# Scores of the first two batches as one float32 product per head half-array, q and k transposed whole

## The chip, the core and the metric

One core of one Trainium2 chip runs the whole program. The metric is the time of one execution on the device in microseconds. The core has a matrix engine (TensorE, PE, with PEld for its weight loads), a vector engine (VectorE, DVE), an activation engine (ScalarE, ACT), a general engine (GpSimd, POOL) and a queue engine that here issues all DMAs (SyncE, SP). Each engine runs its own instructions in the order that the program gives them.

## What is computed

Attention with a top-32 mask, then two dense stages. q, k and v have shape (4, 8, 576, 64): batches, heads, rows, channels.

```
scores = 0.125 * q @ k.T                      # 576 x 576 per batch and head
kth    = the 32nd largest of each row
attn   = softmax over the scores >= kth
x      = attn @ v                             # heads side by side: (4, 576, 512)
# dense stage 1: mixes with the row before, relu(xk @ w_k)^2 @ w_v, times sigmoid(xr @ w_r)
# dense stage 2: gelu(x @ w_in), layer norm of one half, w_sg over the rows, @ w_out, + x
```

The change touches the first line alone, and how q and k get into the layout that it needs.

## The kernel before, in words

**Work and order.** A pair of heads of one batch is a "super" (16 pairs; in batch 0, `HALVED`, each pair is done in two supers of 256 and 320 query rows, so there are 20). A super is cut into slots of 128 query rows; the fifth slot of a pair holds the last 64 rows of both heads. There are 80 slots, 20 to a batch. For each slot the loop at L873 does this: some pieces of preparation for the next super, `emit_S` for the slot two ahead, `emit_topk` for this slot (a search on DVE: L275 and L276 fold a row of 576 into maxima and minima, then MAX8 at L284 and MATCH_REPLACE8 at L294 four rounds), and between its rounds the mask of the slot before (L311), its transposes (`emit_T`) and, at a unit's end, the product with v (`emit_unit`). Into this the dense work of the batch before is spread by a quota, and in slots 0 to 24 the conversion of the float64 weights into pairs of f32r (`conv`, L488 to L497, on ACT, POOL and DVE). A priority is given to each block with `at(...)`, and a list scheduler makes the order of every engine from these. What is left of the dense work of the last batch runs behind the last slot.

**S before.** `load_raw` (L135) brings q and k into `rawq` and `rawk`, in which the blocks 0 to 3 are head 0, 4 to 7 head 1, and 8 the last 64 rows of both. `prep_pieces` (L160) makes the operands: ACT copies to f32r (the high part, L100 and L174), POOL subtracts that from the source (the low part, L102 and L175), so that high and low part of 64 channels fill 128 columns; PE transposes each block (L200, L208, L213, L218), ACT copies the result out of PSUM (L202, L209, L215, L220). `emit_S` (L232) multiplies in two f32r passes over 128 rows (high with both, low with both):

```
for a in range(2):
    for hf in range(2):
        nc.tensor.matmul(ps[:, hf, :HALF], lhsT=su.qst[h, t.u.ch][:, a, ...], rhs=su.kst[h][...], start=(a == 0), stop=(a == 1))
nc.scalar.activation(t.S[:, h].rearrange("p (a n) -> p a n", a=2), ps[:, :, :HALF], AF.Copy)
```

So there are eight products of 288 columns and two copies to a slot, a head at a time, through one PSUM tile (`BUFS["S"] = 1`). The slot with the last rows takes ten products (L253) and one copy (L255). The columns of head 1 are turned by 64, with the remainder first, as the later steps expect.

`split` at L98 is the helper of all high and low parts, of weights (`w`), activations (`xm`, `ksq`, ...) and k (`splk`, `splr`); by its lines L100 and L102 alone they can't be told apart, by the tile names they can.

Of the kernel before, what the change touches and what calls it, by code (L numbers as in the profile page):

```python
# [9 lines left out]
F32 = mybir.dt.float32  # L10
# [3 lines left out]
AF = mybir.ActivationFunctionType  # L14
# [9 lines left out]
def computation(ctx, tc, dram, wscr, flag, fast, q, k, v, mu_k, mu_r, w_k, w_v, w_r, w_in, g_ln, w_sg, b_sg, w_out, out):  # L24
    nc = tc.nc
    B, H, S, D = q.shape
# [7 lines left out]
    HALF = S // 2  # L34

    const = ctx.enter_context(tc.tile_pool(name="const", bufs=1))
    sb = ctx.enter_context(tc.tile_pool(name="sb", bufs=1))
# [65 lines left out]


    HALVED = (0,)

    class Rec:
        pass
# [26 lines left out]
    def load_raw(su, names):  # L135

        b, p = su.b, su.p
        for nm in names:
            if len(nm) == 1:
                nms = [(nm, h, part) for h in range(2) for part in range(2)]  # L140
            else:
                nms = [nm]
            for nm, h, part in nms:
                src = {"q": q, "k": k, "v": v}[nm]
                if nm not in su.raw:
                    su.raw[nm] = sb.tile([128, 9, D], F32, tag="raw" + nm, name="raw" + nm,
                                         bufs=2 if nm == "v" else 1)
                t = su.raw[nm]
                hd = src[b, 2 * p + h]
                if part:  # L150
                    if nm != "q" or 1 in su.chs:
                        nc.sync.dma_start(t[64 * h:64 * h + 64, 8, :], hd[512:])
                elif nm == "q":
                    for c in su.chs:
                        nc.sync.dma_start(t[:, 4 * h + 2 * c:4 * h + 2 * c + 2, :],
                                          hd[256 * c:256 * c + 256].rearrange("(p r) d -> p r d", r=2))
                else:
                    nc.sync.dma_start(t[:, 4 * h:4 * h + 4, :], hd[:512].rearrange("(p r) d -> p r d", r=4))

    def prep_pieces(su):  # L160

        su.kst, su.qst = {}, {}
        pieces = []
        has1 = 1 in su.chs
# [64 lines left out]
    def emit_S(t):  # L232
        su = t.su
        t.S = sb.tile([128, t.hs, S], F32, tag="S2", name="S2", bufs=3)
        for h in range(t.hs):
            ps = bank("S", (128, 2, 512))
            if t.j < 4:
# [596 lines left out]
    for i, t in enumerate(slots):  # L834
        if t.last and t.su.p == NP - 1:
# [3 lines left out]
            elif t.u.ch == 1:  # L839
# [2 lines left out]

    start = at(-100000)
    start.__enter__()
    load_raw(supers[0], [("k", 0, 0), ("q", 0, 0), ("k", 0, 1), ("k", 1, 1), ("k", 1, 0), ("q", 1, 0), ("q", 0, 1),
                         ("q", 1, 1)])
    for pc in prep_pieces(supers[0]):
        pc()
    for key in list(convq)[:4]:
# [138 lines left out]
```

## Time and profile before

| | us |
|---|---|
| median of 3 runs | 1001.49 (997.75 to 1002.79) |
| the profiled execution | 997.91 |
| its span, first to last instruction | 995.8 |
| DVE busy | 841.0 |
| PE busy | 878.1 |
| POOL busy | 528.7 |

The busy times are sums over the span. A slot's search is a run of DVE instructions; the order of the other engines is built around it. PE's busy time is that of pipelined products whose ends are modelled, so that a stretch in which PE is always busy still need not be one at PE's peak; idle time of PE is real. Durations of one form of instruction differ between stretches, which the tables by form show.

### The profile page before, as it was taken

How to read it: one execution, taken by the hardware profiler on the slowest of the kernel's cores; microseconds unless marked ns; L12 is line 12 of the kernel's file. 1: busy time of each engine (PE TensorE's matmuls, PEld its weight loads, DVE VectorE, ACT ScalarE, POOL GpSimd, SP SyncE). 2: the span in 40 equal slices, each digit the busy share in tenths (PEclk: the TensorE clock that was granted, in tenths of full speed). 3: DMA queues.
4: the chain of work that ended last, by engine and by line, in shares of the span. 5: the costliest groups of instructions: out<-in, count | busy, mean ns of one | idle time of the engine just before them, and what ended most of it. 6: DMA issues, size and time to landing. Idle time of an engine off the chain costs nothing.

```text
span 995.8 us, 18647 instructions
## 1 busy us (share of the span) xinstructions
PE 878.1 (88%) x6078; PEld 759.7 (76%) x6078; DVE 841.0 (84%) x2337; ACT 697.6 (70%) x1559; POOL 528.7 (53%) x630
## 2 busy tenths in 40 slices
PE   3465768889888989798999999989999998999997
PEld 2344547777778888577888979868999886899895
DVE  6899999998999999999999999999999973712142
ACT  6778878888886796677687679666876585554340
POOL 7788788675975168559343216598331125210051
PEclk9986779999999999988999999999999999999999
DMA  7953486888467645512333343354333436664432
GB/s 214 371 187 136 156 252 224 282 279 304 167 209 252 219 120 188 171 33 69 109 100 110 110 143 94 99 192 151 109 118 109 128 124 223 218 248 148 122 126 68
DMA packets 105067, 166.34 MB, mean 167 GB/s; under 512 B 19328, under 2 KB 74368, under 8 KB 104960
## 3 DMA queue, kind: packets, MB, share of 16 engines
q1 hardware_dynamic: 104960, 165.05, 50.8%
q8 instruction: 50, 0.82, 0.3%
q14 instruction: 57, 0.47, 0.1%
HBM read 134.27 MB, written 30.21 MB: 165 GB/s over the span
## 4 chain that ended last, share of the span: by engine, by line
PE 45%; DVE 28%; ACT 10%; DMA 8%; POOL 4%; issue 3%; SPq 2%; POOLq 0%; DVEq 0%; ACTq 0%
PE d L569 9%; DVE M L284 8%; PE d L634 6%; DVE E L311 6%; DVE T L294 6%; PE d L679 5%; PE S L240 3%; PE d L760 3%; DVE T L275 3%; PE d L788 3%; PE tp L569 3%; DVE T L276 2%; PE tp L326 2%; PE tp L355 2%; ACT E L306 2%
## 5 line engine op out<-in xcount | busy, mean ns | idle before, releaser
L284 DVE MAX8 M<-T 128x8 f32<-128x208 f32 (+3 forms) x576 | 261.2, 485 | 1.0
L294 DVE MATCH_REPLACE8 T<-M,T 128x208 f32<-128x208 f32 (+2 forms) x432 | 168.9, 394 | 0.0
L569 PE MATMUL d<-xm,w 128*128 128x288 f32 (+2 forms) x1008 | 161.0, 305 | 6.9 <-DMA w<-ws_k 2.4
L311 DVE SCALAR_TENSOR_TENSOR E<-S,M,E 128x576 f32<-128x576 f32 x144 | 147.2, 1048 | 4.7 <-ACT E L306 4.7
L569 PEld LDWEIGHTS d<-xm,w 128*128 128x128 f32 x1008 | 140.5, 191 | 12.5 <-DMA w<-ws_k 3.2
L240 PE MATMUL S<-kst,qst 128*128 128x288 f32 x512 | 111.1, 337 | 28.6 <-ACT S L242 13.6
L240 PEld LDWEIGHTS S<-kst,qst 128*128 128x128 f32 x512 | 83.5, 209 | 41.5 <-ACT S L242 18.9
L326 PE MATMUL tp<-ident,E 128*128 128x128 f32 x512 | 84.6, 295 | 29.2 <-ACT kst L209 14.3
L306 ACT ACTIVATE E<-S,nb 128x576 f32<-128x576 f32 x144 | 105.2, 775 | 0.8
L634 PE MATMUL d<-ksq,w 128*128 128x288 f32 (+2 forms) x672 | 103.9, 302 | 0.6 <-DMA w<-ws_v 0.6
L242 ACT ACTIVATE S<-S 128x576 f32<-128x576 f32 x128 | 83.1, 650 | 30.2 <-DVE E L311 17.4
L326 PEld LDWEIGHTS tp<-ident,E 128*128 128x128 f32 x512 | 64.5, 150 | 38.2 <-ACT kst L209 15.0
L634 PEld LDWEIGHTS d<-ksq,w 128*128 128x128 f32 x672 | 91.8, 189 | 1.6 <-DMA w<-ws_v 0.8
L275 DVE TENSOR_TENSOR T<-S 128x576 f32<-128x576 f32 (+1 forms) x81 | 72.2, 891 | 17.3 <-ACT S L242 12.7
L327 ACT ACTIVATE PT<-tp 128x512 f32<-128x512 f32 x128 | 74.0, 599 | 8.5 <-PE tp L326 8.5
L276 DVE TENSOR_TENSOR T<-S 128x576 f32<-128x576 f32 (+1 forms) x80 | 79.8, 997 | 0.0
L355 PE MATMUL tp<-PT,rawv 128*64 128x256 f32 (+1 forms) x384 | 62.7, 461 | 9.1 <-ACT PT L327 9.1
L760 PE MATMUL d<-w,vn 128*128 128x288 f32 x392 | 60.1, 302 | 5.6 <-DMA w<-ws_sg 2.1
L697 POOL TENSOR_SCALAR bag<-bag 128x1 f32<-128x1 f32 (+1 forms) x20 | 6.1, 303 | 109.5 <-DVE bag L696 108.2
L102 POOL TENSOR_TENSOR ksq<-tmp,ksq 128x576 fp32r<-128x576 f32 (+2 forms) x32 | 41.1, 1289 | 37.3 <-ACT ksq L100 35.4
L760 PEld LDWEIGHTS d<-w,vn 128*128 128x128 f32 x392 | 53.7, 188 | 8.3 <-DMA w<-ws_sg 2.4
L788 PE MATMUL d<-w,gt 128*128 128x512 f32 (+1 forms) x204 | 53.8, 409 | 2.8 <-DVE xr L796 2.5
(182 smaller groups left out, 2018.3 us busy)
## 6 DMA issues: line engine op xcount, KB each, us to landing
w<-ws_k SPq DMA_DIRECT2D x40, 512.0 KB, 3.7
w<-ws_v SPq DMA_DIRECT2D x40, 512.0 KB, 4.1
w<-ws_sg SPq DMA_DIRECT2D x40, 288.0 KB, 3.7
w<-ws_r SPq DMA_DIRECT2D x20, 512.0 KB, 6.2
w<-ws_h SPq DMA_DIRECT2D x20, 512.0 KB, 3.6
w<-ws_u SPq DMA_DIRECT2D x20, 512.0 KB, 3.5
w<-ws_o SPq DMA_DIRECT2D x16, 512.0 KB, 4.6
rawk<-in_k_dram SPq DMA_DIRECT2D x40, 128.0 KB, 2.6
```

Of the source, the lines that this page charges most:

```text
L240: nc.tensor.matmul(ps[:, hf, :HALF], lhsT=su.qst[h, t.u.ch][:, a, 128 * t.i:128 * t.i + 128], rhs=su.kst[h][:, HALF * hf:HALF * hf + HALF] ...
L275: nc.vector.tensor_tensor(T[:, h, :HALF], t.S[:, h, :HALF], t.S[:, h, HALF:], op=OP.max)
L276: nc.vector.tensor_tensor(T[:, :, HALF:], t.S[:, :, :HALF], t.S[:, :, HALF:], op=OP.min)
L284: nc.vector.max(M[:, h, 8 * r:8 * r + 8], src[h][:, seg])
L294: mr = nc.vector.match_replace(L[h][:, seg], M[:, h, 8 * r:8 * r + 8], src[h][:, seg], NEG)
L306: nc.scalar.activation(t.E[:, h], t.S[:, h], AF.Exp, bias=nb[:, h:h + 1], scale=0.125)
L311: m = nc.vector.scalar_tensor_tensor(E, t.S[:, h], t.kv[h], E, op0=OP.is_ge, op1=OP.mult, accum_out=t.u.sums[:, 2 * t.i + h:2 * t.i + h + 1])
L326: nc.tensor.transpose(ps[:, kc, :], E[:, h, 64 * h + 128 * kc:64 * h + 128 * kc + 128], ident)
L569: nc.tensor.matmul(ps[:, :n_], lhsT=w[:, bb, 128 * c:128 * c + 128], rhs=act[ch, which, c][:, a, o:o + n_], start=(c == 0 and i == 0), sto ...
L634: nc.tensor.matmul(ps[:, :nn], lhsT=w[:, bb, 128 * (f % 4):128 * (f % 4) + 128], rhs=kt[f][:, a, o:o + nn], start=(f == 0 and i == 0), sto ...
L760: nc.tensor.matmul(ps[:, :HALF], lhsT=act[b, "vn", i][:, a, 128 * m:128 * m + 128], rhs=W["sg", i, si][:, bb, :HALF], start=(j == 0), stop ...
L788: nc.tensor.matmul(ps[:nn], lhsT=gt[m][:, a, 128 * i:128 * i + nn], rhs=W["o", m][:, bb, :512], start=(j == 0), stop=(j == 11))
```

## The change

`WHOLEF = (0, 1)` names the batches whose S is made in another way; batches 2 and 3 keep the high and low parts. For the two batches:

- `load_raw` puts the two heads' blocks side by side (head h in blocks h, h + 2, ...), so that a transpose of two neighbouring blocks gives the 64 channels of head 0 on partitions 0 to 63 and those of head 1 on 64 to 127.
- `whole_pieces` takes the place of the preparation: float32 transposes straight from the raw tiles, four for k and two for each 256 rows of q, two small ones for the remainders, one ACT copy behind each group. No high or low part is made.
- `emit_S_whole` multiplies in float32 over 64 rows of the array, head 0 with partitions 0 to 63 and head 1 with 64 to 127, both for one half of the columns, then the other; one ACT copy for each half holds both heads. Head 1's first half is two products (64 and 224 columns) since its columns are turned.
- The first loads are in another order and fewer.

```diff
+    WHOLEF = (0, 1)
...
+                if b in WHOLEF and nm != "v" and not part:
+                    if nm == "q":
+                        for c in su.chs:
+                            nc.sync.dma_start(t[:, 4 * c + h:4 * c + h + 3:2, :],
+                                              hd[256 * c:256 * c + 256].rearrange("(p r) d -> p r d", r=2))
+                    else:
+                        nc.sync.dma_start(t[:, h:h + 7:2, :], hd[:512].rearrange("(p r) d -> p r d", r=4))
+                    continue
...
+    def whole_pieces(su):
...
+        def turned(raw, js):
+            ps = bank("tp", (128, 4, 128))
+            for i, j in enumerate(js):
+                nc.tensor.transpose(ps[:, i, :], raw[:, 2 * j:2 * j + 2, :].rearrange("p h d -> p (h d)"), ident)
+            return ps
+
+        def main_k():
+            ps = turned(su.raw["k"], range(4))
+            nc.scalar.activation(su.kT[:, :512], ps.rearrange("p j m -> p (j m)"), AF.Copy)
...
+        def rem():
+            ps = bank("tp", (128, 2, 64))
+            for i, nm in enumerate("kq" if has1 else "k"):
+                raw = su.raw[nm]
+                nc.tensor.transpose(ps[0:64, i, :], raw[0:64, 8, :], ident[0:64, 0:64])
+                nc.tensor.matmul(ps[64:128, i, :], lhsT=raw[64:128, 8, :], rhs=ident[64:128, 64:128], start=True, stop=True)
+            nc.scalar.activation(su.kT[:, 512:], ps[:, 0, :], AF.Copy)
...
+    def emit_S_whole(t):
+        su = t.su
+        for hf in range(2):
+            ps = bank("S", (128, 2, 512))
+            n = HALF * hf
+            for h in range(2):
+                hs = slice(64 * h, 64 * h + 64)
+                if t.j < 4:
+                    lhsT, out_ = su.qT[t.u.ch][hs, 128 * t.i:128 * t.i + 128], ps[:, h]
+                else:
+                    lhsT, out_ = su.qrem[hs], ps[hs, hf]
+                parts = [(0, n, HALF)]
+                if t.j < 4 and h:
+                    parts = [(0, 224, HALF)] if hf else [(0, 512, 64), (64, 0, 224)]
+                for o, ko, m in parts:
+                    nc.tensor.matmul(out_[:, o:o + m], lhsT=lhsT, rhs=su.kT[hs, ko:ko + m], start=True, stop=True)
+            if t.j < 4:
+                nc.scalar.activation(t.S[:, :, n:n + HALF], ps[:, :, :HALF], AF.Copy)
...
-    load_raw(supers[0], [("k", 0, 0), ("q", 0, 0), ("k", 0, 1), ("k", 1, 1), ("k", 1, 0), ("q", 1, 0), ("q", 0, 1),
-                         ("q", 1, 1)])
+    load_raw(supers[0], [("k", 0, 0), ("k", 1, 0), ("q", 0, 0), ("q", 1, 0), ("k", 0, 1), ("k", 1, 1)])
```

How the order of the engines moves, at three places. Lines behind the new code are 72 higher in the changed kernel: L561, L566 and L102 with `w` are steps of the weight conversion there, as L489, L494 and L102 are before; L398 is the transpose L326, L427 to L440 are the product with v (L355 to L368), L641 is the dense product L569.

POOL at the program's start, behind the constants; before:

```order
L102 TENSOR_TENSOR splk<-rawk,splk 128x4x64
L175 TENSOR_TENSOR splq<-rawq,splq 128x2x64
L102 TENSOR_TENSOR splr<-rawk,splr 128x64
L102 TENSOR_TENSOR splk<-rawk,splk 128x4x64
L175 TENSOR_TENSOR splq<-rawq,splq 128x2x64
L489 TENSOR_SCALAR w<-w 128x512 x3
L494 TENSOR_TENSOR w<-w 128x512
L489 TENSOR_SCALAR w<-w 128x512
L102 TENSOR_TENSOR splk<-rawk,splk 128x4x64
```

and now:

```order
L561 TENSOR_SCALAR w<-w 128x512 x3
L566 TENSOR_TENSOR w<-w 128x512
L561 TENSOR_SCALAR w<-w 128x512
L566 TENSOR_TENSOR w<-w 128x512
L102 TENSOR_TENSOR w<-w 128x512
L566 TENSOR_TENSOR w<-w 128x512
```

The splits of k, q and their remainders are gone, and POOL begins with the weights.

PE at the program's start, the first super's operands and first products; before:

```order
L208 MATMUL tp<-identr,splk 128x128 x4
L200 MATMUL tp<-identr,splq 128x128 x4
L240 MATMUL S<-kst,qst 128x288
L208 MATMUL tp<-identr,splk 128x128 x4
L200 MATMUL tp<-identr,splq 128x128 x4
L213 MATMUL tp<-identr,splr 128x128
L240 MATMUL S<-kst,qst 128x288 x15
```

and now:

```order
L178 MATMUL tp<-ident,rawk 128x128 x4
L178 MATMUL tp<-ident,rawq 128x128 x2
L197 MATMUL tp<-ident,rawk 64x64
L198 MATMUL tp<-ident,rawk 64x64
L221 MATMUL S<-kT,qT 128x288
L221 MATMUL S<-kT,qT 128x64
L221 MATMUL S<-kT,qT 128x224
L221 MATMUL S<-kT,qT 128x288 x3
```

17 transposes and the first products of one head became eight transposes, all ahead of the first product, which needs both heads' operands.

PE where dense work runs beside the slots (the product with v of a unit with the last rows, then S); before:

```order
L355 MATMUL tp<-PT,rawv 64x320 x8
L569 MATMUL d<-xm,w 128x256 x8
L361 MATMUL tp<-ident,rinv 64x128 x4
L366 MATMUL tp<-PTr,rawv 64x320
L368 MATMUL tp<-ident,rinv 64x64
L366 MATMUL tp<-PTr,rawv 64x320
L368 MATMUL tp<-ident,rinv 64x64
L240 MATMUL S<-kst,qst 128x288 x3
L569 MATMUL d<-xm,w 128x256 x2
L240 MATMUL S<-kst,qst 128x288
```

and now:

```order
L427 MATMUL tp<-PT,rawv 64x320 x8
L433 MATMUL tp<-ident,rinv 64x128 x4
L438 MATMUL tp<-PTr,rawv 64x320
L440 MATMUL tp<-ident,rinv 64x64
L438 MATMUL tp<-PTr,rawv 64x320
L440 MATMUL tp<-ident,rinv 64x64
L221 MATMUL S<-kT,qT 128x288
L221 MATMUL S<-kT,qT 128x64
L221 MATMUL S<-kT,qT 128x224
L641 MATMUL d<-xm,w 128x256 x7
```

A group of S is now the two heads for one half of the columns (three products, or two in the other half), between products that use the whole array. The order behind the last slot is the same in both programs.

## Rows read from the trace of the kernel before

**Rows 1.** The page: DVE's busy time and its tenths in 40 slices

```profile
PE 878.1 (88%) x6078; PEld 759.7 (76%) x6078; DVE 841.0 (84%) x2337; ACT 697.6 (70%) x1559; POOL 528.7 (53%) x630
DVE  6899999998999999999999999999999973712142
```

**Rows 2.** Windows by stage: length; PE, PEld, DVE, ACT, POOL busy; clock; DMA share

```profile
0.00:12.00 12.00, 4.55 (x23) 3.80 (x24) 3.10 (x8) 7.55 (x17) 6.29 (x22) 1.00 0.71 228
12.00:207.00 195.00, 133.16 (x857) 105.61 (x857) 190.77 (x514) 156.48 (x375) 159.78 (x176) 0.88 0.70 230
207.00:418.00 211.00, 191.12 (x1336) 163.77 (x1334) 201.49 (x567) 165.08 (x371) 134.67 (x157) 0.97 0.63 209
418.00:831.00 413.00, 394.89 (x2851) 346.05 (x2852) 391.72 (x1149) 300.86 (x657) 192.63 (x224) 0.97 0.37 117
831.00:996.00 165.00, 154.33 (x1018) 140.48 (x1016) 53.91 (x104) 67.63 (x143) 35.30 (x53) 0.99 0.49 161
```

**Rows 3.** Waits of DVE from 12 to 418: total us, times, longest

```profile
DVE x L420 <- ACT rb L413: 4.9, 3, 2.2
DVE T L275 <- ACT S L242: 2.6, 1, 2.6
```

**Rows 4.** POOL by form, 0 to 415: count, busy us, mean ns, idle before

```profile
L102 POOL TENSOR_TENSOR splk<-rawk,splk 128x256 fp32r<-128x256 f32 x27 | 24.9, 922 | 6.2 <-ACT splk L100 6.2
L175 POOL TENSOR_TENSOR splq<-rawq,splq 128x256 fp32r<-128x256 f32 x11 | 11.5, 1043 | 4.9 <-ACT splq L174 3.8 <-DMA vn<-vsTrue 1.1
L175 POOL TENSOR_TENSOR splq<-rawq,splq 128x128 fp32r<-128x128 f32 x16 | 10.3, 643 | 0.4 <-ACT splq L174 0.2
L102 POOL TENSOR_TENSOR splr<-rawk,splr 128x64 fp32r<-128x64 f32 x13 | 6.8, 519 | 0.1
L175 POOL TENSOR_TENSOR splr<-rawq,splr 128x64 fp32r<-128x64 f32 x9 | 4.8, 538 | 3.5 <-ACT splr L174 3.5
```

**Rows 5.** DVE by form, 0 to 415: count, busy us, mean ns

```profile
L311 DVE SCALAR_TENSOR_TENSOR E<-S,M,E 128x576 f32<-128x576 f32 x67 | 69.1, 1059 | 0.0
...
L276 DVE TENSOR_TENSOR T<-S 128x576 f32<-128x576 f32 x32 | 35.7, 1116 | 0.0
L275 DVE TENSOR_TENSOR T<-S 128x576 f32<-128x576 f32 x31 | 30.0, 967 | 4.4 <-ACT S L242 2.6
```

**Rows 6.** DVE by form from 720 to 800, and that window's busy times

```profile
L311 DVE SCALAR_TENSOR_TENSOR E<-S,M,E 128x576 f32<-128x576 f32 x15 | 14.0, 955 | 0.0
...
L276 DVE TENSOR_TENSOR T<-S 128x576 f32<-128x576 f32 x7 | 6.5, 926 | 0.0
...
L275 DVE TENSOR_TENSOR T<-S 128x576 f32<-128x576 f32 x7 | 5.4, 778 | 2.6 <-ACT S L242 2.3
...
720.00:800.00 80.00, 80.00 (x584) 71.47 (x583) 75.45 (x244) 51.83 (x119) 17.26 (x19) 1.00 0.36 115
```

**Rows 7.** Timeline of PE, 160 to 186: start us, length us, array x columns, count

```profile
159.95 2.37 PE L355 MATMUL tp<-PT,rawv 128*64 128x320 f32 x16
...
168.46 0.68 PE L240 MATMUL S<-kst,qst 128*128 128x288 f32 x4
...
175.23 0.46 PE L208 MATMUL tp<-identr,splk 128*128 128x128 f32 x4
...
175.87 1.39 PE L253 MATMUL S<-kst,qrem 128*128 128x288 f32 x10
...
183.93 0.60 PE L334 MATMUL tp<-ident,E 128*128 128x128 f32 x4
184.46 0.24 PE L338 MATMUL tp<-ident,E 64*64 64x64 f32 x1
184.63 0.33 PE L339 MATMUL tp<-ident,E 64*64 64x64 f32 x2
184.89 0.67 PE L240 MATMUL S<-kst,qst 128*128 128x288 f32 x3
```

**Rows 8.** Timeline of DVE: the first instruction of the first search

```profile
11.49 0.46 DVE L275 TENSOR_TENSOR T<-S 128x288 f32<-128x288 f32 x1 [0.79 <-ACT S L242]
```

More of the change, by code (lines that the diff above doesn't have):

```diff
@@ L158, in load_raw, with main_q @@
                     nc.sync.dma_start(t[:, 4 * h:4 * h + 4, :], hd[:512].rearrange("(p r) d -> p r d", r=4))
+    def whole_pieces(su):
+        su.kT = sb.tile([128, S], F32, tag="kst", name="kT", bufs=4)
+        su.qT = {}
+        has1 = 1 in su.chs
+        def turned(raw, js):
[6 more added lines that the diff above has]
+            nc.scalar.activation(su.kT[:, :512], ps.rearrange("p j m -> p (j m)"), AF.Copy)
+        def main_q():
+            nch = len(su.chs)
+            ps = turned(su.raw["q"], [2 * c + i for c in su.chs for i in range(2)])
+            t = sb.tile([128, 2, 256], F32, tag="qst", name="qT", bufs=4)
+            nc.scalar.activation(t[:, :nch], ps.rearrange("p (c i) m -> p c (i m)", i=2)[:, :nch], AF.Copy)
+            for i, c in enumerate(su.chs):
+                su.qT[c] = t[:, i, :]
+        def rem():
[5 more added lines that the diff above has]
+            nc.scalar.activation(su.kT[:, 512:], ps[:, 0, :], AF.Copy)
+            if has1:
+                su.qrem = sb.tile([128, 2, 256], F32, tag="qst", name="qR", bufs=4)[:, 0, :D]
+                nc.scalar.activation(su.qrem, ps[:, 1, :], AF.Copy)
+        return [main_k, main_q, rem]
@@ new lines, in emit_S_whole @@
+    def emit_S_whole(t):
[16 more added lines that the diff above has]
+                nc.scalar.activation(t.S[:, :, n:n + HALF], ps[:, :, :HALF], AF.Copy)
+            else:
+                nc.scalar.activation(t.S[:, 0, n:n + HALF], ps[:, hf, :HALF], AF.Copy)
@@ L160, in prep_pieces @@
     def prep_pieces(su):
+        if su.b in WHOLEF:
+            return whole_pieces(su)
         su.kst, su.qst = {}, {}
@@ L234, in emit_S @@
         t.S = sb.tile([128, t.hs, S], F32, tag="S2", name="S2", bufs=3)
+        if su.b in WHOLEF:
+            emit_S_whole(t)
+            return
         for h in range(t.hs):
```

## The prediction

> **What bounds the kernel now.** I read the share of busy time first: VectorE (DVE) works 841 of the 995.8 us, and its 40 slices stand at 9 or 8 from the second to the 32nd [rows 1]. The table by stage says where that holds. I cut at 12 us (the first search), at 207 and 418 (between them stand the S products of batch 1), and at 831 (the last mask). DVE is busy 190.8 of 195 us in the stage of batch 0's S and 201.5 of 211 in batch 1's; TensorE (PE) is busy 133.2 and 191.1 there. From 418 to 831 both are near full (PE 394.9, DVE 391.7 of 413), and behind 831 PE does the rest alone, 154.3 of 165 us [rows 2]. So the end is a tail of PE work behind the last search, and the search is a line of DVE work; where the change lies, up to 418, DVE sets the pace with hardly a wait: the two largest between 12 and 418 are 4.9 us before L420 (on an ACT copy) and 2.6 us before L275 (on a copy of S) [rows 3]. Anything that shortens DVE's line before 418 moves all that follows, since the program order of the tail is the same in both kernels. Anything put on PE costs nothing until PE's 19.9 idle us in the stage of batch 1 are used up.
>
> **DVE.** Its instructions are the same in kind and number in both programs. Their lengths are not fixed. Two-input instructions run longer where GpSimd (POOL) is busy: up to 415 us, with POOL at 300.7 of 418 us (72%), L311 takes 1059 ns, L276 1116, L275 967 [rows 2, 5]; from 720 to 800, with POOL at 17.26 of 80 (22%), the same forms take 955, 926 and 778 [rows 6]. The change takes from POOL every split of q and k of 12 pairs: 24 of k (0.92 us each), 16 of q with 128 columns (0.64) and 8 with 256 (1.04), 12 remainders of k (0.52) and 8 of q (0.54) [rows 4], whose counts hold some of batch 2's too. That is 22.1 + 10.3 + 8.3 + 6.2 + 4.3 = 51 us, or 12 points of POOL's share of 418 us. The differences between the stages are 67 x 0.104 + 32 x 0.190 + 31 x 0.189 = 19 us for 50 points; 12 points give **4.6 us, taken as 5**. Bounds: nothing, if POOL's remaining work (weight conversion) moves up and meets the same DVE instructions; 9 us, if each of the 68 split instructions costs DVE the 0.13 us that the three differences average.
>
> A split can cost more than its share. If a two-input DVE instruction that meets a split has to stand until it ends, the mean loss is half a split, 0.46 us. The three forms fill 134.8 of some 400 busy us [rows 5], so a third of the 68 splits meet one at any moment, and somewhat more do over their whole length: about 10 us. The Trainium skill ("SBUF — State Buffer", on the shared port pair) says just this: DVE and GpSimd lock the pair for a whole instruction, DVE also when it has two SBUF inputs, and the other blocks; by it the term would be 10 instead of 5. The trace agrees that only such forms stretch, but the means stretch by 0.1 to 0.2 us; I take the rows and keep the rest as a rival.
>
> **PE.** Before, a slot's S is two groups (a head each) of four f32r products of 288 columns, 0.68 us a group end to end, 0.53 by its spacing (0.13 each) [rows 7]. Now it is two groups (a half of the columns each, both heads), and a head's float32 product runs as two passes. Float32 passes of 320 columns in L355 come in pairs on the two column halves: 16 in 2.37 us less the last one's tail, 0.27 a pair; scaled to 288 that is 0.24, so **0.49 us** a group if the heads run side by side, 0.97 if one follows the other. No row of before shows row halves with all 128 columns; L355 is the nearest, so I take 0.49 and keep 0.97. To this comes the change of array shape. Where 64x64 products stand between full ones, L338 and L339 (three passes, 64 columns, about 0.05 each) fill 0.43 us from 184.46 to 184.89, and the three products after them take 0.67 instead of about 0.56; I book **0.3 us** in and out. The Trainium skill ("TensorEngine Tiling (Array Packing)", Key Properties) speaks against the change here: a change of tiling mode drains TensorE. The trace agrees, with that 0.3; without it the groups would come out 17 us cheaper in all. A group thus goes from 0.53 to 0.79, +0.26: 64 groups, +17 us, half of it in each stage. The remainder slot goes from 1.39 us (ten products, L253) to two groups of 0.79: +0.2, eight times. Transposes come out even: 17 to 27 in f32r at 0.07 (L208) against 6 to 8 in float32 at 0.11 (L334) with one or two remainder pieces like L338 with L339 (0.43). PE's sum: about +19 us, of which +9 between 207 and 418, under 19.9 us of idle time. Cost on the path: **0**, with a bound of +10 below.
>
> **ACT, DMA, start.** ACT loses the copies of the splits and half of those behind the transposes; S is copied by as many elements. Where a DVE wait goes: the two of [rows 3] are on ACT copies; I take **2 us** of their 7.5, bounds 0 and 7.5, and what is late next is PE's product. The raw loads carry the same bytes in pieces of 256 bytes, through as many issues on SP; DMA's share of 0.63 to 0.70 leaves room [rows 2], cost 0 to 1 us at the start only. The first search waits for S until 11.49 us [rows 8]. The new path has no split and no subtraction, but its first half needs both heads' k and q and the remainder of k, and ACT has a weight conversion ahead of the first copy of S: **1 us** less, bounds 3 less and 1 more.
>
> **Sum:** 5 + 2 + 1 = 8 us less than the profiled execution's 997.9, which is 989.9. That execution lies 3.6 us under the median of the runs (1001.5); from the median it is **993.5**.
>
> **Rivals.**
> - *PE becomes the bound in the stage of batch 1, slower.* If a group's heads run one after the other, that stage's PE work grows by 9 + 32 x 0.48 = 24 us: 191.1 + 24 = 215 in 211. PE's waits for others don't all go; with a quarter of its idle time left (5) the stage lasts 220, +9, less the 3 or 4 us won before it: +6, **1007**. It decides from about 1.15 us a group, where the idle time is used up (0.53 + 19.9 / 32). For it: no row shows the row halves; against: the column halves of L355 do run in pairs.
> - *POOL's time was not what held DVE, about the same.* Conversion work fills the gap (POOL's first new rows are all conversion), the 5 us stay, and PE's 9 us use up the waits that ACT gives back: -2, **999.5**.
> - *The splits block whole instructions*, 10 us, and the waits give 3: -14, **987.5**.
>
> **How the numbers follow.** Forecast 0.52, rival PE 0.17, same 0.20, blocking 0.11. What a measurement tells from no change is 0.5%, 5 us. The forecast's own range is 989 to 998, and a seventh of it lies within 5 us of before. Faster: 0.45 + 0.11 + 0.01 = 0.57; same: 0.07 + 0.17 + 0.04 = 0.28; slower: 0.13 + 0.02 = 0.15. The range runs from 984 (blocking, with all of the waits gone) to 1006, short of the PE rival's middle.
>
> **What would show it.** Right: the mask of the last slot ends some 8 us earlier than 831 and the tail behind it is as long; L311, L276 and L275 are shorter up to 415 and unchanged from 720 to 800; passes of the two heads start within some 10 ns of each other. Wrong: DVE waits for S copies between 207 and 418 while PE has no idle time there (PE rival); the three forms are as long as before (same). A tail of another length behind the last mask, or a granted clock that falls below the 0.88 and 0.97 of the first two stages, would be an error of another kind: I left both as they are.

## The result and the profile after

The changed kernel takes **1010.19 us** (median of 6 runs, 1008.79 to 1012.30); the kernel before took 1001.19 us beside it (997.18 to 1002.79). The ratio is 1.0101, 95% interval 1.0081 to 1.0121: 8 to 12 us slower, where 8 us less had been forecast. The profiled execution took 1012.30 us (span 1010.6). It is the slowest of the six, and the profiled one of before (997.91) lies 3 us under its median: the two spans differ by 14.8 us where the change costs some 10. What is read below from single executions is good to some us only.

The page of the changed kernel: busy time, instructions, and DVE's tenths, which answer to [rows 1].

```profile
PE 898.5 (89%) x6014; PEld 740.4 (73%) x6014; DVE 839.0 (83%) x2337; ACT 667.2 (66%) x1459; POOL 482.9 (48%) x562
DVE  5999999998989988999999999899988973612143
```

ACT has 30 us less to do and POOL 46 (51 had been counted); PE has 20 more. DVE's work is the same, 839 us, but its slices hold more 8s in the first half than in [rows 1]. The windows by stage, as in [rows 2], with the last one longer:

```profile
0.00:12.00 12.00, 5.34 (x19) 3.36 (x19) 3.07 (x7) 4.24 (x7) 3.65 (x17) 1.00 0.65 200
12.00:207.00 195.00, 138.19 (x814) 94.82 (x815) 190.12 (x499) 136.53 (x308) 130.94 (x131) 0.82 0.73 235
207.00:418.00 211.00, 194.56 (x1266) 148.77 (x1265) 191.90 (x563) 149.89 (x328) 111.53 (x132) 0.96 0.61 197
418.00:831.00 413.00, 391.46 (x2811) 340.68 (x2813) 389.94 (x1141) 297.78 (x655) 190.32 (x214) 0.98 0.37 115
831.00:1010.00 179.00, 168.95 (x1112) 152.75 (x1106) 63.99 (x130) 78.77 (x164) 46.45 (x70) 0.98 0.50 162
```

Between 207 and 418 DVE is busy 191.9 us instead of 201.5: nearly 10 us more idle time, in the stage where it set the pace. (The windows lie at fixed times; the changed kernel is some 8 us further back in its program there, so the marks below are the better measure.) Its waits between 190 and 400 (in all us, times, longest), the changed kernel:

```profile
DVE x L492 <- PE tp L438: 6.2, 2, 3.5
DVE T L347 <- ACT S L223: 3.4, 3, 1.8
DVE x L492 <- ACT rb L485: 3.1, 2, 2.0
DVE bst L767 <- ACT vraw L606: 2.9, 1, 2.9
DVE tmp L714 <- PE d L706: 2.7, 4, 1.6
```

These five come to 18.3 us. The same stretch of before has the 4.9 us of [rows 3] and three single waits of 1.3, 1.1 and 0.5. The waits are for PE products, and for ACT copies of them. The first search (L347), which began at 11.49 us in [rows 8], begins at 14.42, in the timeline of DVE:

```profile
14.42 1.12 DVE L347 TENSOR_TENSOR T<-S 128x288 f32<-128x288 f32 x1 [2.20 <-ACT S L223]
```

The last mask ends at 844.2 us instead of 830.3; behind it the span goes on for 166.4 us (165.5 before). The tail is the same, as foreseen; the loss is in DVE's line ahead of it.

To compare stretches I mark each slot by the start of its second search instruction (L276 in before). The table is worked out from the traces of single executions: DVE's time at five marks, the span, and, up to slot 79, DVE's idle time and the time in the two-input instructions of the three lines of [rows 5], those on half a row (128x288) among them, each without its overlap with the instruction before.

```
kernel     slot 4   20     40     60     79    span  | DVE idle  two-input
before      67.4  232.0  433.3  619.8  819.4   995.8 |   39.9     282.1
after       65.3  239.8  441.0  628.1  833.3  1010.6 |   56.0     279.2
newload     68.0  240.7  441.5  630.1  831.5  1006.1 |   46.5     284.2
nosub       62.7  232.7  431.3  615.9  817.8   991.9 |   43.9     275.2
f32r        64.1  238.5  442.0  626.7  830.0  1003.5 |   47.1     283.0
bigT        66.2  237.8  438.5  627.7  825.7  1001.3 |   49.7     274.2
```

The changed kernel loses 10 us between slots 4 and 20, in batch 0, and 6 more between 60 and 79, where its S is made as before, having been 2 us ahead at slot 4. Between slots 20 and 40, in batch 1, it loses nothing (201.2 us against 201.3): DVE waits 5.5 us longer there, and the two-input instructions on whole rows take 67.7 us instead of 73.3. Up to slot 79 its two-input instructions take 2.9 us less and its waits 16.1 us more. The 2.9 us lie in the instructions on half a row; those on whole rows, the forms of [rows 5], take 273.5 us before and 273.9 after. (newload, nosub, f32r and bigT are experiments, below.)

### The profile page after: what moved, and what is told of

Read it like the earlier page. It is cut to its first block, busy times and chain, and to the rows that moved or that the text cites. A ratio compares the mean times of both kernels' runs of the same rounds, so it can differ in the third digit from the quotient of the medians.

```text
span 1010.6 us, 18219 instructions
## 1 busy us (share of the span) xinstructions
PE 898.5 (89%) x6014; PEld 740.4 (73%) x6014; DVE 839.0 (83%) x2337; ACT 667.2 (66%) x1459; POOL 482.9 (48%) x562
## 4 chain that ended last, share of the span: by engine, by line
PE 41%; DVE 32%; ACT 9%; DMA 7%; POOL 5%; issue 4%; SPq 1%; DVEq 0%; POOLq 0%; ACTq 0%
DVE M L356 9%; PE d L641 8%; DVE E L383 7%; DVE T L366 7%; PE d L706 6%; PE d L751 4%; DVE T L347 3%; PE tp L641 3%; DVE T L348 3%; PE d L860 2%; PE tp L427 2%; PE d L832 2%; PE S L312 2%; PE tp L398 2%; ACT E L378 2%
## 5 line engine op out<-in xcount | busy, mean ns | idle before, releaser
L641 PE MATMUL d<-xm,w 128*128 128x288 f32 (+2 forms) x1008 | 168.4, 314 | 5.7 <-POOL xm L102 2.4
L641 PEld LDWEIGHTS d<-xm,w 128*128 128x128 f32 x1008 | 146.7, 199 | 14.4 <-issue 4.1
L398 PE MATMUL tp<-ident,E 128*128 128x128 f32 x512 | 85.4, 297 | 36.0 <-DVE E L383 30.6
L398 PEld LDWEIGHTS tp<-ident,E 128*128 128x128 f32 x512 | 64.5, 151 | 48.5 <-DVE E L383 31.2
L347 DVE TENSOR_TENSOR T<-S 128x576 f32<-128x576 f32 (+1 forms) x81 | 69.9, 864 | 24.3 <-ACT S L314 13.4
L221 PE MATMUL S<-kT,qT 64*128 64x288 f32 (+2 forms) x320 | 62.7, 457 | 21.3 <-ACT S L223 18.8
L348 DVE TENSOR_TENSOR T<-S 128x576 f32<-128x576 f32 (+1 forms) x80 | 77.7, 972 | 0.0
L427 PE MATMUL tp<-PT,rawv 128*64 128x256 f32 (+1 forms) x384 | 67.2, 467 | 3.0 <-ACT PT L399 1.7
L566 POOL TENSOR_TENSOR w<-w 128x512 int32<-128x512 int32 x32 | 44.7, 1396 | 39.5 <-ACT w L565 19.5
L102 POOL TENSOR_TENSOR ksq<-tmp,ksq 128x576 fp32r<-128x576 f32 (+2 forms) x32 | 41.0, 1283 | 43.1 <-ACT ksq L100 43.0
L221 PEld LDWEIGHTS S<-kT,qT 64*128 64x128 f32 x320 | 31.5, 209 | 38.3 <-ACT S L223 24.9
L751 PE MATMUL d<-w,x 128*128 128x512 f32 (+1 forms) x216 | 56.2, 408 | 1.3 <-DMA w<-ws_h 1.3
```

Of the source, the lines that this page charges most:

```text
L221: nc.tensor.matmul(out_[:, o:o + m], lhsT=lhsT, rhs=su.kT[hs, ko:ko + m], start=True, stop=True)
L347: nc.vector.tensor_tensor(T[:, h, :HALF], t.S[:, h, :HALF], t.S[:, h, HALF:], op=OP.max)
L348: nc.vector.tensor_tensor(T[:, :, HALF:], t.S[:, :, :HALF], t.S[:, :, HALF:], op=OP.min)
L398: nc.tensor.transpose(ps[:, kc, :], E[:, h, 64 * h + 128 * kc:64 * h + 128 * kc + 128], ident)
L641: nc.tensor.matmul(ps[:, :n_], lhsT=w[:, bb, 128 * c:128 * c + 128], rhs=act[ch, which, c][:, a, o:o + n_], start=(c == 0 and i == 0), sto ...
L751: nc.tensor.matmul(ps[:nn], lhsT=act[ch, 2, c][:, a, o:o + nn], rhs=W["h", c][:, bb, :512], start=(j == 0), stop=(j == 11))
```

## The experiments

All ratios are to the kernel before, timed on the same chip beside them, with 95% intervals.

### The load alone, and GpSimd's subtractions alone

`newload` is the kernel before with the changed loads, and the splits reading the new places:

```
+                if b < 2 and nm != "v" and not part:
+                    if nm == "q":
+                        for c in su.chs:
+                            nc.sync.dma_start(t[:, 4 * c + h:4 * c + h + 3:2, :], ...)
+                    else:
+                        nc.sync.dma_start(t[:, h:h + 7:2, :], ...)
```

> The kernel before with one part of the change alone: the raw q and k rows of the first two batches land in pieces of 256 bytes with the two heads alternating, as in the changed kernel, and are then split in hi and lo parts as before. If the smaller pieces are behind the early loss of batch 0 (later landings, or slower weight streams in a stretch whose DMA share is 0.70), this kernel takes 1004 us or more and DVE reaches the twentieth slot 3 us or more later than in the kernel before (232 us). If the load is free, as the prediction's DMA term of 0 to 1 says, it takes 1000 to 1002.5.

Measured: **1007.78 us** (1005.48 to 1010.46), ratio 1.0072 [1.0044, 1.0101], 7 us more with PE, ACT and POOL doing the same work; slot 20 is reached at 240.7 us, as late as in the changed kernel (239.8). The load is not free, as the first case expected. A window that I had not read, 12 to 60 us (columns as in [rows 2]), in the kernel before and in newload:

```profile
12.00:60.00 48.00, 22.84 (x96) 17.41 (x97) 44.70 (x113) 33.97 (x74) 38.91 (x39) 1.00 0.95 310
```

```profile
12.00:60.00 48.00, 21.98 (x87) 16.20 (x86) 44.96 (x113) 33.72 (x70) 36.30 (x37) 1.00 0.95 313
```

The share of 0.70 of the whole stage [rows 2] is a mean: while the first weights come in, the DMA engines are busy for 0.95, and there is little room. But newload has the same share there and moves as many bytes (313 GB/s against 310), so this window doesn't show by itself how the finer pieces cost time. By the packet records (medians) 1 KB takes 46 ns, 512 bytes 27 and 256 bytes 18, so a row of 1 KB in four pieces takes 72 ns. The Trainium skill ("DMA: Bandwidth & Descriptors", Specifications) names 512 bytes as the least transfer for line rate; the trace agrees in part: 256 bytes are the slowest, with 14 bytes per ns, but 512 reach 19 and 1 KB 22. SyncE, which issues all loads in order, also needs longer for each; its timeline in before and then in newload:

```profile
0.78 0.40 SPq L158 DMA_DIRECT2D rawk<-in_k_dram  x1
1.24 0.41 SPq L155 DMA_DIRECT2D rawq<-in_q_dram  x1
...
4.04 2.08 SPq L452 DMA_DIRECT2D raw<-in_moe_w_r_dram  x4
```

```profile
0.78 0.70 SPq L156 DMA_DIRECT2D rawk<-in_k_dram  x1
1.54 0.61 SPq L153 DMA_DIRECT2D rawq<-in_q_dram  x1
...
4.79 2.25 SPq L460 DMA_DIRECT2D raw<-in_moe_w_r_dram  x4
```

The first block of weights lands at 9.1 us instead of 7.9, the 13th at 37.1 instead of 34.7, the 21st at 63.2 instead of 58.6. Their conversion on ACT, POOL and DVE then falls on other DVE work. The masks from 60 to 245 us (mean in ns before the last bar), in before, newload and after:

```profile
L311 DVE SCALAR_TENSOR_TENSOR E<-S,M,E 128x576 f32<-128x576 f32 x30 | 29.6, 1011 | 0.0
```

```profile
L319 DVE SCALAR_TENSOR_TENSOR E<-S,M,E 128x576 f32<-128x576 f32 x30 | 34.1, 1158 | 0.0
```

```profile
L383 DVE SCALAR_TENSOR_TENSOR E<-S,M,E 128x576 f32<-128x576 f32 x30 | 33.9, 1159 | 0.0
```

The load alone stretches these masks as much as the whole change does, by 4.4 us. That the later weights are the link between load and masks is read from the order of these events, not tested by itself, and other traces speak against it: in bigT (below), with the old loads, the 13th block lands at 37.1 us too and these masks take 1067 ns; in fill, with the old loads and all of POOL's splits, they take 1101. The cost of the load is shown, its mechanism is open.

`nosub` is the kernel before with ACT's copy in place of POOL's subtraction, in the first two batches (shown for q; k and the remainders likewise):

```
+            if su.b < 2:
+                nc.scalar.activation(sp[:, :n], src[:, :, None, :].to_broadcast([128, n, 3, D]), AF.Copy)
+                return
             nc.scalar.activation(sp[:, :n, 0::2, :], ...)
             nc.gpsimd.tensor_tensor(sp[:, :n, 1, :], ..., op=OP.subtract)
```

> The kernel before without GpSimd's subtractions in the first two batches: ScalarE copies the same values into the low part too, so the product there is that of the high parts twice over and its low part is left out. The products, transposes and loads stay. GpSimd loses about 45 us. By the prediction's stretch term DVE's two-input instructions shorten and the kernel takes 995 to 999 us. By the rival that GpSimd's time was not what held DVE, it takes 1000 to 1002. If the freed GpSimd lets weight conversions land under DVE's masks and that is the loss of batch 0, DVE is later at the twentieth slot than in the kernel before (232 us), by 3 us or more.

Measured: **992.86 us** (987.76 to 996.29), ratio 0.9912 [0.9881, 0.9944]: 6 to 12 us less, more than the 2 to 6 that were expected. The prediction's largest term is there, and larger than booked. By form, 0 to 415 us, as in [rows 5]:

```profile
L320 DVE SCALAR_TENSOR_TENSOR E<-S,M,E 128x576 f32<-128x576 f32 x68 | 75.5, 1138 | 1.8 <-ACT E L315 1.8
L285 DVE TENSOR_TENSOR T<-S 128x576 f32<-128x576 f32 x32 | 29.7, 927 | 0.0
L284 DVE TENSOR_TENSOR T<-S 128x576 f32<-128x576 f32 x31 | 27.8, 898 | 1.8
```

The two search forms fall from 1116 and 967 ns to 927 and 898; the masks rise from 1059 to 1138: what POOL now does earlier seems to meet them. Up to slot 79 the two-input instructions take 6.9 us less (table), about half of it on half rows. The trace is of an execution 3.9 us shorter than that of before, the medians differ by 7.8; where the rest is, one execution doesn't tell. nosub also takes a step out of the way to the operands: up to 420 us the transposes of before wait 11.6 us for POOL's splits (L200 7.4, L208 4.2), and 4.7 us of nosub's gain are there by slot 4. What each of the two gives was not tried apart. Slot 20 comes at 232.7 us, so the third case of the expectation doesn't hold by its mark. But the masks are longer in nosub too, and its slots 4 to 20 take 5.3 us more than in before; that conversions under the masks cost batch 0 time is not excluded.

### The load undone within the change

`bigT` is the changed kernel with the old loads. The blocks of the two heads then lie four apart, and each is turned by itself:

```
-                if b in WHOLEF and nm != "v" and not part:
+                if False:
...
-                nc.tensor.transpose(ps[:, i, :], raw[:, 2 * j:2 * j + 2, :].rearrange("p h d -> p (h d)"), ident)
+                nc.tensor.transpose(ps[0:64, i, :], raw[:, j, :], ident)
+                nc.tensor.matmul(ps[64:128, i, :], lhsT=raw[:, 4 + j, :], rhs=ident, start=True, stop=True)
```

> The changed kernel with the loads of the kernel before: each head's rows in pieces of 1 KB (k) and 512 bytes (q). [...] The finer load alone cost the kernel before 7 us. If it costs the changed kernel as much and the turning of halves costs TensorE nothing on the path, this takes 1002 to 1004 us; if the halves cost 0.3 us of TensorE per pair (128 more of them, 38 us, of which about half on the path as for the other added TensorE work), 1015 us or more; if the finer load was only a matter of the order in the kernel before, 1009 to 1012.

Measured: 1007.79 us (1003.03 to 1011.76), ratio 1.0073 [1.0046, 1.0100], some 2 to 3 us less than the changed kernel, between the cases and within the noise of the two intervals. Its page says why it can't show the load's 7 us clean:

```profile
PE 927.2 (93%) x6174; PEld 745.9 (74%) x6174; DVE 837.4 (84%) x2337; ACT 665.3 (66%) x1459; POOL 478.4 (48%) x562
```

PE is busy 28.7 us longer than in the changed kernel, nearly all of it ahead of slot 40, and the kernel is still no slower. If the load gives back its 7 us here too, those 29 us cost about 5, a sixth; that is an estimate, since no run shows what the load costs within the change. `bigT4` has also the dense steps 4 slots late instead of 5 (below).

> The same with the dense steps 4 slots late instead of 5 from slot 19 on, which gave the changed kernel 7.5 us (1002.75 us) and the kernel before 1.5 (999.38). If the two gains add up, 995 to 998 us, below both kernels; if they are the same time gained in two ways, 1002 to 1004; if the halves cost TensorE time on the path, 1006 or more.

Measured: 1006.35 us (1004.45 to 1009.18), ratio 1.0058 [1.0038, 1.0077], at the edge of the third case. The two gains don't add up.

### The product, made shorter and longer

`f32r` is the changed kernel with kT and qT stored as f32r, so that a product of a full slot is one pass instead of two; it leaves out the low part of that product. The slots with the last rows read the same kT as float32.

```
-        su.kT = sb.tile([128, S], F32, tag="kst", name="kT", bufs=4)
+        su.kT = sb.tile([128, S], F32R, tag="kst", name="kT", bufs=4)
-            t = sb.tile([128, 2, 256], F32, tag="qst", name="qT", bufs=4)
+            t = sb.tile([128, 2, 256], F32R, tag="qst", name="qT", bufs=4)
```

> The changed kernel with the products of the full slots in one f32r pass over the 64 rows in the place of two float32 passes (it leaves out the low part of the product; the remainder slots stay float32): a group is about 0.3 us of streaming shorter, the array's shape still changes twice. Theory A: the loss goes and DVE's shorter line shows, 994 to 1000. Theory B: as the changed kernel, 1006 to 1011.

Measured: 1004.58 us (1002.20 to 1007.11), ratio 1.0040 [1.0021, 1.0059]. That is between the two theories: without the second pass the time is some 6 us shorter. PE's busy time falls by 26.1 us (898.5 to 872.4), below that of the kernel before (878.1), so f32r takes out more than the change had put in, and a quarter of it comes through. By the marks nothing is gained up to slot 40 (442.0 us against 441.0), where all of the shortened products lie; the gain comes behind it.

`fill` is the kernel before with two more products in each group of S of the first two batches, whose results the true ones overwrite:

```
+                if su.b in (0, 1):
+                    for hf in range(2):
+                        nc.tensor.matmul(ps[:, hf, :HALF], lhsT=su.qst[h, t.u.ch][:, 0, 128 * t.i:128 * t.i + 128],
+                                         rhs=su.kst[h][:, HALF * hf:HALF * hf + HALF], start=True, stop=True)
```

> The kernel before, with two more f32r products of 288 columns in each S group of batches 0 and 1 (their result is overwritten): 0.26 us of PE work more a group, 64 groups, as the prediction booked for the changed kernel, and nothing else changed. Theory A: PE's load alone makes DVE wait, 1006 to 1010. Theory B: PE has the idle time for it, 1000 to 1003.

Measured: 1007.46 us (1002.32 to 1011.33), ratio 1.0070 [1.0045, 1.0095]. As theory A has it: PE's busy time rises by 11.9 us (878.1 to 890.0), that of the S products alone, counted without overlap, by 17.9, and the time by 7. So of work put into the groups of S about half comes through here, and a quarter in f32r. Where it comes through, the traces don't show: the profiled execution of fill, the fastest of its nine, is 3.1 us ahead of before at slot 40 (430.2 us), behind the last added product, and 6.8 us behind it at slot 79.

### One batch at a time

`b0only` and `b1only` change one batch and leave the other as before:

```
-    WHOLEF = (0, 1)
+    WHOLEF = (0,)      # b0only;  (1,) in b1only
```

> The new S for batch 0 alone; batches 1 to 3 as before. Theory A (PE's load: the changed kernel's loss of some 9 us comes from PE's longer S groups in the stretch where dense work runs beside the slots, from 207 us on): batch 0's slots lie where PE has idle time, so nothing is lost there and DVE gains the 2 or 3 us of shorter two-input instructions: 997 to 1000 against 1001. Theory B (the scheduler's other order and a lower granted clock early in the program, 61 us at half clock before 130 us against 39, whatever PE's passes cost): the early stretch is as in the changed kernel, so 3 to 6 us of the loss are there: 1004 to 1007.

> The new S for batch 1 alone; batch 0 as before. Theory A: all of the loss is here, 1007 to 1011 against 1001. Theory B: the early stretch is as before, so under half of the loss is left, 1001 to 1005.

Measured: 1007.72 us (1005.39 to 1009.23), ratio 1.0073 [1.0049, 1.0097], and 1007.66 us (1006.22 to 1010.20), ratio 1.0071 [1.0046, 1.0097]. Each half of the change alone costs 7 us, both together 10, not 14. In the profiled executions b0only is 6.7 us behind the kernel before at slot 20 and no further behind at slot 40 or 79 than 9; b1only is level up to slot 40 and loses 7 us between slots 40 and 60, behind the last changed product, and 4 more up to 79. The loss is not one place's, and neither theory holds for both runs: A fails on b0only, B on b1only.

### The order of the dense work

A first set asked whether the kernel before only has a lucky order, which any rebuild would lose. The quota of dense steps per slot (0.995) was set to 0.99 and 0.98, in the kernel before (`bq099`, `bq098`) and after (`aq099`, `aq098`):

```
-        quota = 0.995 * dense.left() / (nxt - s)
+        quota = 0.99 * dense.left() / (nxt - s)
```

> The kernel before with the dense work's quota at 0.99 in the place of 0.995: the same instructions, another order. Theory C (the order of the kernel before is a good one among many, and any other build of the same work loses some microseconds of DVE waits and of stretched two-input instructions): 1003 to 1008 against 1001, with no instruction changed. Theory A (PE's load): 999 to 1003, no change.

> The kernel before with the quota at 0.98, a second draw of the order. Theory C: 1003 to 1008. Theory A: 999 to 1004.

> The changed kernel with the quota at 0.99. Theory C: the changed kernel is one draw from a spread of several microseconds, so this one may come out anywhere from 1001 to 1012, and the mean over the draws is nearer to that of the kernels before with the same quotas than 9 us. Theory A: 1008 to 1012, as the changed kernel.

> The changed kernel with the quota at 0.98, another draw. Theory C: 1001 to 1012. Theory A: 1008 to 1013.

Measured: before 1001.23 and 1000.73 us, ratios 0.9996 [0.9977, 1.0016] and 0.9999 [0.9983, 1.0015]; after 1010.62 and 1008.67, ratios 1.0110 [1.0073, 1.0146] and 1.0095 [1.0057, 1.0132]. Theory C fails for these orders: the kernel before keeps its time, and the changed kernel its loss.

Then the slot in which dense steps come due, from slot 19 on, was moved from 5 slots late to 4 or 6 (`bs4`, `bs6` before; `as4`, `as6` after), and to 3 (`as3`):

```
-        with at(1000 * (s + (2 if s < 19 else 5)) + 500):
+        with at(1000 * (s + (2 if s < 19 else 4)) + 500):
```

> The kernel before with dense work put 4 slots late in the place of 5 from slot 19 on: the same instructions, an order that differs far more than with the other quotas (PE's sequences agree to 0.72 against 0.92). Theory C, in the form that the small changes of the quota leave open (an order that was found for this work is lost by any large rebuild): 1004 to 1008. Theory A (what PE has to do): 999 to 1003.

> The kernel before with dense work 6 slots late from slot 19 on (PE's sequences agree to 0.88). Theory C: 1004 to 1008. Theory A: 999 to 1003, with more dense work left behind the last slot.

> The changed kernel with dense work 4 slots late from slot 19 on. Theory A: 1008 to 1012, as before the shift. Theory C: another draw, 1002 to 1012.

> The changed kernel with dense work 6 slots late from slot 19 on, so that PE's slot work has less dense work ahead of it. Theory A: DVE's waits from 20 to 40 shrink and the tail grows by about as much, 1007 to 1012. Theory C: 1002 to 1012.

> The changed kernel with the dense steps due 3 slots late from slot 19 on, where it has 5 (4 took 1002.75 us). If each slot by which the dense work comes earlier moves TensorE work from the stretch after the last mask into idle time of TensorE that the changed kernel still has, it gains again, 1000 to 1003 us. If 4 is where the cover ends, the waits of DVE grow in slots 40 to 79 as TensorE fills up, and it takes 1004 to 1010.

Measured: before, 999.38 us at 4 (ratio 0.9990 [0.9964, 1.0017]) and 1001.36 at 6 (1.0014 [0.9990, 1.0037]). After, **1002.75 us at 4** (1.0032 [1.0014, 1.0049]), 1009.05 at 6 (1.0097 [1.0065, 1.0130]), 1007.17 at 3 (1.0067 [1.0041, 1.0093]). For the kernel before theory C fails again; for the changed kernel as4 falls outside theory A's range, and as3 is in that of its second case. as6 also clears the granted clock, 0.82 from 12 to 207 in the changed kernel and 0.88 before: as6 has 0.88 there and still takes 1009 us, and nosub, the fastest of all, has 0.75. At 4 the changed kernel gets 7 us back, at 3 it loses half of them: the tail behind the last mask grows shorter still, but in the profiled execution the waits of DVE up to slot 79 rise to 72 us. bigT4, with the same 4, hardly gains, so the 7 us hang on this one order. In as4 the last mask ends 2.6 us earlier than in the changed kernel and the tail is 7.3 us shorter; in bs4 the tail is 8.5 us shorter than in before, but the last mask ends 12.5 us later (single executions). Why as4 keeps the gain of the tail I can't say.

### GpSimd's work put back

`poolback` is the changed kernel with 43 us of dead subtractions on POOL, where the splits had been (POOL busy 519.9 us instead of 482.9):

```
+        def sub(nm, lo, hi):
+            d = sb.tile([128, 4, 2, D], F32R, tag="splk", name="splk", bufs=1)
+            r = su.raw[nm][:, lo:hi, :]
+            nc.gpsimd.tensor_tensor(d[:, :hi - lo, 1, :], r, r, op=OP.subtract)
```

> The changed kernel with GpSimd's subtractions put back as dead work of the same shapes at the same places (their results are not used). GpSimd gets back about 45 us. If the stretch term is right, this costs 4 to 6 us: 1014 to 1017 us. If conversions that land under the masks are the loss of batch 0, it takes 1004 to 1008. If GpSimd has no part in it, 1009 to 1012.

Measured: 1021.56 us (1018.32 to 1026.34), ratio 1.0215 [1.0183, 1.0247], 11 us more than the changed kernel and outside all three ranges. It doesn't give the size of the stretch: its trace has one wait of DVE (in us, times, longest) that is longer than that.

```profile
DVE x L504 <- ACT rb L497: 17.8, 1, 17.8
```

The next raw q may be loaded only when POOL has read the old one, and SyncE waits for that, until 105.4 us (total, times, longest, from 95 to 140 us):

```profile
SPq L154 <- POOL splk L174: 4.7, 1, 4.7
```

Several more waits on POOL's weight conversions follow on SyncE, so that a weight load goes out at 130.5 us only and lands at 135.1. ACT's conversion of it stands ahead of the copy (rb) for which DVE waits until 136.7. This is read from the chain of waits, not tested by itself. SyncE issues its loads in order, so that what it waits for here holds up the loads behind.

## Why the prediction was wrong

**The DVE stretch, -5: right in kind; too small for nosub, too large for the changed kernel.** Without POOL's subtractions the time falls by 9 us (nosub), near the rival of whole instructions blocked, of which the rows show 7 us in two-input time. In the changed kernel most of it is not there: up to slot 79 these instructions take 2.9 us less, none of it on whole rows. By form up to 415 us only one of the three is shorter, against [rows 5]:

```profile
L383 DVE SCALAR_TENSOR_TENSOR E<-S,M,E 128x576 f32<-128x576 f32 x66 | 68.4, 1065 | 0.5 <-ACT E L378 0.5
...
L348 DVE TENSOR_TENSOR T<-S 128x576 f32<-128x576 f32 x31 | 34.7, 1118 | 0.0
L347 DVE TENSOR_TENSOR T<-S 128x576 f32<-128x576 f32 x30 | 27.3, 910 | 5.3 <-ACT S L223 3.7
```

**"DMA's share of 0.63 to 0.70 leaves room", cost 0 to 1 us at the start: the first step that failed, by 7 us.** newload, the kernel before with nothing but the changed load, takes 7 us more. The term was read from means over 195 and 211 us; the window from 12 to 60 us, which could have been read beforehand, shows 0.95. How the load costs its time is open, and so is how much of it the changed kernel pays: bigT, which undoes the load there, gains no more than 2 to 3 us.

**"Cost on the path: 0", PE's 9 us under 19.9 idle: the second; its size is open, up to about 6 us.** PE's sum came out as counted, 19 forecast and 20.4 measured; how much of the match is luck can't be told. Counted without overlap, the products of S take 8.1 us more where 19 were booked, the transposes of q and k 4.6 less where they were to come out even, and the products that are the same in both kernels 16.9 more. The traces don't tell how much of the last is the change of the array's shape at each group, which was booked with S, and how much the granted clock (118 us of the span at its lower level, 1.2 GHz, against 92 before). A group of S was booked at 0.79 us; the timeline of PE, as [rows 7], has 0.76 for four passes, with the next product 0.69 us behind the group's start, and 0.87 where the second head comes in two pieces:

```profile
161.29 0.87 PE L221 MATMUL S<-kT,qT 64*128 64x288 f32 x6
...
165.49 0.76 PE L221 MATMUL S<-kT,qT 64*128 64x288 f32 x4
166.18 1.11 PE L641 MATMUL d<-xm,w 128*128 128x256 f32 x7
```

The heads do run side by side, their first passes 7 ns apart, so the rival of PE as the bound by serial heads falls, although the time ends near its 1007. What failed is the cover: fill adds PE work where PE had idle time, and 7 us come of it. An engine that works in order has its idle time in front of particular instructions; work that is put ahead of another one delays that one, idle time elsewhere or not. That reading fits fill, but the traces don't show it at its place: the slots 20 to 40 are no longer than before, and fill and b1only lose their time behind slot 40, where S is made as before. PE's idle time ahead of the products of S did not grow either; before, over all four batches (24.3 us of it up to 420 us), and after, for the changed products alone:

```profile
L240 PE MATMUL S<-kst,qst 128*128 128x288 f32 x512 | 111.1, 337 | 28.6 <-ACT S L242 13.6 <-ACT qst L202 11.0 <-ACT S L255 2.4
```

```profile
L221 PE MATMUL S<-kT,qT 64*128 64x288 f32 (+2 forms) x320 | 62.7, 457 | 21.3 <-ACT S L223 18.8 <-ACT qT L189 2.5
```

The bound of +10 that I kept for this was the right order; I took 0. f32r speaks for a limit to this step: with less PE work than the kernel before, and POOL relieved as in nosub against the load's 7 us, it is still 4 us slower.

**The waits, -2, and the start, -1: both of the other sign.** DVE's waits grew by 16 us up to slot 79. The first search starts 2.9 us later instead of 1 earlier; newload has 1.3 of these (12.75 us). f32r, with the same loads and the same need of both heads, starts it at 10.18. What differs is ACT's order. In the changed kernel the products of the second half are done at 11.3 us, but a weight conversion that waits for its load stands ahead of their copy (ACT's timeline):

```profile
12.64 0.66 ACT L560 ACTIVATE w<-raw 128x512 f32<-128x512 f32 x1 [1.84 <-DMA raw<-in_moe_w_r_dram]
13.20 0.65 ACT L565 ACTIVATE w<-raw 128x512 int32<-128x512 uint32 x1
13.75 0.64 ACT L223 ACTIVATE S<-S 128x576 f32<-128x576 f32 x1
```

The prediction had seen such a conversion and set its bound at 1 us more. In f32r the two copies come at 8.14 and 9.49 us, with one conversion between them that doesn't wait. The start is not the loss: at slot 4 the changed kernel is 2 us ahead of before.

**The tail** was left as it was, rightly; the transposes, left even, came out 4.6 us cheaper and were not tried alone. The granted clock, left as it was, fell from 0.88 to 0.82, which as6 and nosub show not to be the loss. Two sums of the prediction are off without moving the forecast: 64 times 0.3 us is 19 us and not 17, and the three differences average 0.145 us over their instructions and not 0.13.

**The sum of the parts.** -8.8 (nosub), +7.2 (newload) and +6.1 (second pass, after less f32r) make +4.5 of the measured +10.1 (ratios against about 1000 us). Each has an interval of about 3 us to either side, and they need not add; 6.1 is too much for the product, since f32r takes out more than was put in. So 6 us or more of the loss stay open, with an error of some 5. Candidates are the change of the array's shape at each group, the two heads' joint group, which makes the first head wait for the second, and the order of the dense work, which moves the changed kernel by 7 us and the kernel before by 2. No run separated them. No complete version ran faster than the kernel before: bs4, at 0.9990, is the same.

## What to carry to other kernels

Read the share of a queue in windows as short as the bursts of its transfers, and run a changed load alone: a mean of 0.70 held 48 us at 0.95, and a load of the same bytes in finer pieces cost 7 us. Idle time of an in-order engine is no sure cover for added work: 12 us more of PE's busy time in the groups of S cost 7 us, 29 us more in transposes made a pair of heads ahead cost perhaps 5 (an estimate). Compare stages by marks in the program and not by windows of time: the window from 207 to 418 us showed 10 us more idle time of DVE, and the slots of that batch took as long as before. And when a change trades one thing for another, run each side alone: here the half that was aimed at, taking work from POOL, gains 9 us by itself, and the load that came along costs 7 by itself.

## What was not expected of the hardware

- Passes of the two row halves (64 rows by 128 columns each, float32, 288 columns) start 7 ns apart, their second passes 347 ns behind the first, and a full product follows 333 ns behind the last of them: 0.69 us a group. At the rate of L355's pairs in [rows 7] the passes alone would take 0.48 (an estimate).
- A DMA packet of 256 bytes takes 18 ns against 27 for 512 bytes and 46 for 1 KB, and an issue on SyncE of 128 KB in 256-byte pieces 0.70 us against 0.40 in pieces of 1 KB.
- Taking 50 us of subtractions from POOL (528.7 to 478.6 us busy) shortened a kernel whose DVE is nearly always busy by 6 to 12 us; up to 415 us DVE's two search forms were shorter by 0.07 and 0.19 us each, and the masks longer by 0.08.
